# Six instead of seven gate tiles in the first phase of an S5 + SwiGLU kernel

## The chip, the cores and the metric

The kernel runs on one core of one Trainium2 chip. The metric is device time in microseconds of one execution; the time before is the median of three runs. One execution was also profiled, and all readings of the trace come from that one.

## The reference, cut to what matters

For x of 1 x 2048 x 512 in bf16, the kernel computes a layernorm and two branches on it, a state-space scan (S5) and a SwiGLU feed-forward with F = 1376:

```python
xn = _layernorm(x, axis=-1)
return x + _A_ref(xn, ...) + _B_ref(xn, w_gate, w_up, w_down)
# _B_ref
g = _silu(x @ w_gate)
u = x @ w_up
return (g * u) @ w_down
```

`_A_ref` multiplies xn by a complex matrix (512 x 512), runs the recurrence h = Lam_bar * h + Bu along the 2048 tokens, multiplies by C, and adds xn * Dskip. What the change touches is the gate product of the first 512 tokens and the layernorm of these tokens.

## The kernel before, in words

The tokens are cut into four chunks of 512, and a chunk into four token tiles of 128. F is cut into ten tiles of 128 and a rest of 96; tiles go in pairs (`FP`, L710), so a chunk has five gate pairs and five up pairs. Each pair takes a pair of PSUM banks: two times four matmuls of 512 columns (one for each 128 rows of the contraction, `ffn_mm`, L714) fill it, and one instruction of ScalarE (ACT) reads it, a silu for gate (`silu_pair`, L726) or a copy for up (`ffn_up`, L779). There are eight banks, so four pairs. `next_pair` (L374) hands them out in rotation: it skips a pair that is reserved, and one in which TensorE (PE) has written and nobody is yet recorded as its reader (`_bank_live`, L369).

The work is put down as tasks with the tiles that they read and write, and a planner makes the order when the program is built. PE and the DMA queue of SyncE (SP) keep the order in which the code adds their tasks (`_CHAIN`). ACT, VectorE (DVE) and GpSimd (POOL) are sorted by a list planner (`_schedule`) by estimated times (`est`), with extra orders where `order` or `od` gives them. Waits follow from the tiles; a bank counts as a whole, so a task that writes a bank waits for all who read it before.

The first phase handles chunk 0 while x and the weights are still coming in; later chunks get their transposes by DMA and are not touched. `ffn_gate_quarters([0, 1, 2, 3])` (L742) does this:

- Four bank pairs are reserved for eight gate tiles. The last bank (7) is taken off the list for transposes (`xt_pair`, L746); seven tiles remain, in banks 0 to 6. Gate tile 6's bank also takes warm-up matmuls on constants (`pe_warm`) and the first transpose.
- `ln_chunk0` (L513) puts one chain on DVE for token tiles 0 to 3: statistics of 128x512 (L517), aggregate (L518), then a root on ACT (L519), reciprocal (L524), and xn (`ln_apply`, L500). Before tile 3's reciprocal stands a small transpose of parameters (L522).
- `xt_tile` (L543) transposes xn of a token tile on PE in four blocks of 128 (L548) and copies them to `xnT`: on ACT in three copies for tiles 0 to 2 (L559), on DVE in two for tile 3 (L557). Tile 1's blocks are transposed two and two, into the same bank 7; tiles 2 and 3 in one go of four.
- For each token tile q, the k slices (contraction rows) are taken in groups, and within a group all seven gate tiles get a matmul of 128 columns for each slice (L763). The table `place` (L754) says ahead of which of these the transposes of the next token tile stand. Tile q = 3 goes in two groups of two slices.
- ACT's order of roots and copies is written out (`seq`, L769): sd0, ev0_0, ev0_1, sd1, ev0_2, ev1_0, ev1_1, sd2, ev1_2, ev2_0, ev2_1, sd3, ev2_2 (sd is a root, ev a copy of transposes). Then ACT loads the silu table (`act_table`, L772).
- Gate tile 7 follows as four 512-column matmuls in bank 7 (L774), then the four silu pairs are put down.

After it the code adds three up pairs of chunk 0, the fifth gate pair, two more up pairs, and the rest of the kernel. The first up pair takes banks 0 and 1, which the first silu reads.

The gate weights come as four loads, one for each k slice, of the columns of the first-phase tiles (`wg_load`, L424; `FG = NQ * 128`, L416), two on SP's queue (slices 1 and 3) and two on ACT's (0 and 2). The other gate columns come in one load (`ld_wg1`, L441) on SP behind the first up load. `wres` (L705) makes a gate tile from number `NQ` on wait for that load.

Of the kernel before, what the change touches and what calls it, by code (L numbers as in the profile page):

```python
# [14 lines left out]
AF = mybir.ActivationFunctionType  # L15
# [235 lines left out]
def bass_parallel_sum__ssm_conv_s5__swiglu_ffn__prompt_kernel(  # L251
# [28 lines left out]
    EPS = 1e-5  # L280

    g = _Graph()
    es = ExitStack()
    with es:
# [9 lines left out]
        x_sb = sb("x_sb", [128, NT, D], B16)  # L294
# [33 lines left out]
        st = sb("st", [128, 8, 6], F32)  # L328
# [45 lines left out]
        def next_pair():  # L374
            for _ in range(NB // 2):
                b = 2 * (pair_ctr[0] % (NB // 2))
                pair_ctr[0] += 1
                if not (b in reserved or _bank_live(b) or _bank_live(b + 1)):
                    return b
            raise AssertionError("all PSUM pairs live")  # L380
# [31 lines left out]

        TILEB = 128 * D * 2
        FH0 = 6 * 128
        NQ = 7
        FG = NQ * 128  # L416

        def pload(name, slot, src, **kw):
# [54 lines left out]
        def pe_warm(n, w=512, bk=None):  # L473
            if bk is None:
                bk = next_pair()

            def mm(e, bk=bk):
                for _ in range(n):
                    inst = e.matmul(pbank[:, bk, 0:w], lhsT=one.to_broadcast([128, 128]), rhs=one.to_broadcast([128, w]), start=True, stop=True)  # L479
                return inst  # L480
            g.add("pe", mm, writes=BK(bk), name="pe_warm", est=n * w * 0.84, ninst=n)
# [17 lines left out]
        def ln_apply(a, order=()):  # L499
            return g.add("dve", lambda e: e.tensor_scalar(out=xn_sb[:, a % NXN, :], in0=x_sb[:, a, :], scalar1=mv[:, a, 0:1], scalar2=rstd[:, a:a + 1],  # L500
                                                          op0=ALU.subtract, op1=ALU.mult),
                         reads=[("x", a), ("mv", a), ("rstd", a)], writes=[("xn", a % NXN)], name="xn%d" % a, est=350, order=order)
# [8 lines left out]
        hold = {}  # L511

        def ln_chunk0():  # L513
            last = None
            for a in range(4):
                order = (last,) if last else ()
                last = g.add("dve", lambda e, a=a: e.bn_stats(out=st[:, a, :], in_=x_sb[:, a, :]), reads=[("x", a)], writes=[("st", a)], name="bnst%d" % a, est=640, order=order)  # L517
                last = g.add("dve", lambda e, a=a: e.bn_aggr(out=mv[:, a, :], in_=st[:, a, :]), reads=[("st", a)], writes=[("mv", a)], name="bnag%d" % a, est=160, order=(last,))  # L518
                hold["sd%d" % a] = g.add("act", lambda e, a=a: e.activation(out=sd0[:, a:a + 1], in_=mv[:, a, 1:2], func=AF.Sqrt, bias=EPS),  # L519
                                         reads=[("mv", a)], writes=[("sd0", a)], name="sd%d" % a, est=190)  # L520
                if a == 3:
                    last = g.add("dve", lambda e: e.transpose(out=prT[:], in_=prow[:]), reads=[("prow", k) for k in range(3)] + [("prow0",)],  # L522
                                 writes=[("praw", k) for k in range(3)], name="parT", est=90, order=(last,))
                last = g.add("dve", lambda e, a=a: e.reciprocal(out=rstd[:, a:a + 1], in_=sd0[:, a:a + 1]), reads=[("sd0", a)], writes=[("rstd", a)],  # L524
                             name="rstd%d" % a, est=140, order=(last,))
                last = ln_apply(a, (last,))
            hold["xn3"] = last

        def ln_chunk(c):
            for a in range(4 * c, 4 * c + 4):  # L530
# [7 lines left out]
                for a in range(4 * c, 4 * c + 4):  # L538
                    ln_apply(a)

        xt_pair = [None]

        def xt_tile(a, k0, k1, slot=None):  # L543
            slot = xt_pair[0] if slot is None else slot

            def tr(e):
                for k in range(k0, k1):
                    inst = e.transpose(out=ptr[:, slot, k * 128:(k + 1) * 128], in_=xn_sb[:, a, k * 128:(k + 1) * 128], identity=ident[:])  # L548
                return inst
            g.add("pe", tr, reads=[("xn", a), ("ident",)], writes=BK(slot), name="xT%d_%d" % (a, k0), est=(k1 - k0) * 64, ninst=k1 - k0)  # L550
            src = ptr[:, slot, 0:512].rearrange("p (k t) -> p k t", k=KT)
            for q0, q1 in ((0, 2), (2, 4)) if a == 3 else ((0, 1), (1, 2), (2, 4)):
                if q0 < k0 or q1 > k1:
                    continue
                rd = dict(reads=BK(slot), writes=[("xnTq", a, k) for k in range(q0, q1)] + ([("xnT", 0, a)] if q1 == KT else []), name="xTev%d_%d" % (a, q0))
                if a == 3:
                    t = g.add("dve", lambda e, q0=q0, q1=q1: e.tensor_copy(out=xnT[0][:, a, q0:q1, :], in_=src[:, q0:q1]), est=320, order=(hold["xn3"],), **rd)  # L557
                else:
                    t = g.add("act", lambda e, q0=q0, q1=q1: e.activation(out=xnT[0][:, a, q0:q1, :], in_=src[:, q0:q1], func=AF.Identity), est=130 + 110 * (q1 - q0), **rd)  # L559
                hold["ev%d_%d" % (a, q0)] = t  # L560
# [153 lines left out]
        def ffn_mm(c, i, which, bk):  # L714
            fs = fsz[i]
            w = wg if which == "g" else wu

            def mm(e, bk=bk, w=w, i=i, fs=fs, c=c):
                for kt in range(KT):
                    inst = e.matmul(pbank[0:fs, bk, :].rearrange("p (j t) -> p j t", j=4), lhsT=w[:, kt, i * 128:i * 128 + fs], rhs=xnT[c][:, :, kt, :],  # L720
                                    start=(kt == 0), stop=(kt == KT - 1))
                return inst
            g.add("pe", mm, reads=wres("wg" if which == "g" else "wu", i) + [("xnT", c, j) for j in range(4)],
                  writes=BK(bk), name="mm_%s%d_%d" % (which, c, i), est=4 * 216, ninst=4)
# [10 lines left out]
        def ffn_gate(c, ip):  # L735
            i0, n = FP[ip]
            bk = next_pair()
            for k in range(n):
                ffn_mm(c, i0 + k, "g", bk + k)
            silu_pair(c, ip, bk)  # L740

        def ffn_gate_quarters(pairs):  # L742
            banks = {ip: next_pair() for ip in pairs}
            reserved.update(banks.values())
            tiles = [(2 * ip + k, banks[ip] + k) for ip in pairs for k in range(2)]
            xt_pair[0] = tiles.pop()[1]  # L746
            wbank = tiles[-1][1]
            pe_warm(8, 512, wbank)
            pe_warm(2, 128, wbank)
            ln_chunk0()  # L750
            xt_tile(0, 0, 1, wbank)
            xt_tile(0, 1, 4)
            pe_warm(1, 256, tiles[-2][1])
            place = {(0, 2, 4): (1, 0, 2), (1, 0, 3): (1, 2, 4), (1, 2, 2): (2, 0, 4), (2, 2, 2): (3, 0, 4)}  # L754
            for q in range(4):
                for k0, k1 in (((0, 1), (1, 2), (2, 3), (3, 4)), ((0, 1), (1, 2), (2, 4)), ((0, 1), (1, 2), (2, 4)), ((0, 2), (2, 4)))[q]:
                    for n, (i, bk) in enumerate(tiles):
                        if (q, k0, n) in place:
                            xt_tile(*place[(q, k0, n)])

                        def mm(e, bk=bk, i=i, q=q, k0=k0, k1=k1):
                            for kt in range(k0, k1):
                                inst = e.matmul(pbank[:, bk, q * 128:(q + 1) * 128], lhsT=wg[:, kt, i * 128:(i + 1) * 128], rhs=xnT[0][:, q, kt, :],  # L763
                                                start=(kt == 0), stop=(kt == KT - 1))
                            return inst
                        g.add("pe", mm, reads=[("wg", "k%d" % k) for k in range(k0, k1)] + [("xnTq", q, k) for k in range(k0, k1)], writes=BK(bk),
                              name="mm_gq%d_%d_%d" % (i, q, k0), est=(k1 - k0) * 56, ninst=k1 - k0)
            reserved.clear()
            seq = ["sd0", "ev0_0", "ev0_1", "sd1", "ev0_2", "ev1_0", "ev1_1", "sd2", "ev1_2", "ev2_0", "ev2_1", "sd3", "ev2_2"]  # L769
            for a_, b_ in zip(seq, seq[1:]):  # L770
                hold[b_].od.add(hold[a_])
            act_table(AF.Silu, (hold["ev2_2"],))  # L772
            hold["evac"] = g.tasks[-1]
            ffn_mm(0, NQ, "g", xt_pair[0])  # L774
            for ip in pairs:
                silu_pair(0, ip, banks[ip])
            hold["evac"] = [t for t in g.tasks if t.name == "silu0_0"][0]

        def ffn_up(c, ip):  # L779
            i0, n = FP[ip]  # L780
# [180 lines left out]
            dc_A(c0 + 1, 3, 416, 96, bk)  # L961
            dc_B(c0 + 1, 3, 416, 96, bk, 1)

        ffn_gate_quarters([0, 1, 2, 3])
        params_a()
        tables()
        params_b()
# [91 lines left out]
```

## Time and profile before

| what | value |
|---|---|
| median of 3 runs | 178.13 us (177.83 to 178.2) |
| the profiled execution | 178.16 us |
| its span, first to last instruction | 176.3 us |
| busy: PE, DVE, ACT, POOL | 98%, 92%, 47%, 6% |
| first-phase matmuls (L763) | 112, of 128 columns each, 5.3 to 12.9 us |
| first silu (L732) | starts at 12.53 us |
| later gate and up matmuls (L720) | 512 columns, from 12.89 us on |

All times within the trace count from the start of the span. A line of the timeline has the start, the duration, the engine (PEld is PE's weight load), the line of the code, the operation, the output and inputs by name, the shape, how many instructions are merged, and in brackets the idle time before with what ended it. `pb` is a PSUM bank, `wgu` the gate and up weights, `sg` the silu's output, `st`, `mv`, `sd`, `rstd` the steps of the layernorm. The chain of waits is the work that ended last, followed back from the end: at each step what released it. A line of it has start, duration, engine, tile and line.

### The profile page before, as it was taken

How to read it: one execution, taken by the hardware profiler on the slowest of the kernel's cores; microseconds unless marked ns; L12 is line 12 of the kernel's file. 1: busy time of each engine (PE TensorE's matmuls, PEld its weight loads, DVE VectorE, ACT ScalarE, POOL GpSimd, SP SyncE). 2: the span in 40 equal slices, each digit the busy share in tenths (PEclk: the TensorE clock that was granted, in tenths of full speed). 3: DMA queues.
4: the chain of work that ended last, by engine and by line, in shares of the span. 5: the costliest groups of instructions: out<-in, count | busy, mean ns of one | idle time of the engine just before them, and what ended most of it. 6: DMA issues, size and time to landing. Idle time of an engine off the chain costs nothing.

```text
span 176.3 us, 2474 instructions
## 1 busy us (share of the span) xinstructions
PE 173.0 (98%) x954; PEld 85.7 (49%) x962; DVE 161.7 (92%) x279; ACT 83.6 (47%) x113; POOL 10.8 (6%) x21
## 2 busy tenths in 40 slices
PE   8999999999999999999999999999999999999995
PEld 2894444444444496444444444444444444444443
DVE  2773999999999999999999999999999999999933
ACT  3469989799999767100356564000265620000000
POOL 3040500127000000000000000000000000000000
PEclk9999999999999999999999999999999999999999
DMA  5996665654685101023240000001100000000122
GB/s 162 272 372 163 129 125 172 154 115 86 119 289 121 32 0 30 4 60 100 54 130 0 4 0 0 0 0 59 63 0 0 0 0 0 0 4 0 59 89 89
DMA packets 26246, 13.48 MB, mean 76 GB/s; under 512 B 18460, under 2 KB 26108, under 8 KB 26236
## 3 DMA queue, kind: packets, MB, share of 16 engines
q1 hardware_dynamic: 25916, 12.89, 27.5%
q10 hardware_dynamic: 320, 0.46, 0.7%
q8 instruction: 7, 0.11, 0.3%
q14 instruction: 3, 0.02, 0.0%
HBM read 6.85 MB, written 2.10 MB: 51 GB/s over the span
## 4 chain that ended last, share of the span: by engine, by line
PE 96%; ACT 1%; ACTq 1%; issue 1%; DVE 0%
PE pb L720 36%; PE pb L908 19%; PE pb L837 16%; PE pb L922 16%; PE pb L763 4%; PE pb L802 3%; PE pb L919 1%; PE pb L954 1%; ACTq L405 1%; ACT L468 1%; PE pb L548 1%; DVE xn_sb L500 0%; ACT sm L468 0%; DVE x_sb L926 0%; PE pb L479 0%
## 5 line engine op out<-in xcount | busy, mean ns | idle before, releaser
L720 PE MATMUL pb<-xnT,wgu 128*128 128x512 bf16 x212 | 46.2, 379 | 0.0
L877 DVE TENSOR_TENSOR_SCAN rot<-sm,car,rot 128x512 bf16<-128x512 f32 x32 | 38.8, 1266 | 0.0
L732 ACT ACTIVATE sg<-pb 128x1024 bf16<-128x1024 f32 x20 | 20.1, 1023 | 34.9 <-PE pb L720 33.8
L908 PE MATMUL pb<-wd,hT 128*128 128x512 bf16 (+2 forms) x166 | 34.5, 366 | 0.2
L720 PEld LDWEIGHTS pb<-xnT,wgu 128*128 128x128 bf16 x212 | 20.7, 98 | 24.8 <-ACT sg L732 0.2
L922 PE MATMUL pb<-W,hss 128*128 128x512 bf16 (+2 forms) x132 | 28.6, 366 | 0.3 <-issue 0.2
L908 PEld LDWEIGHTS pb<-wd,hT 128*128 128x128 bf16 x170 | 16.2, 98 | 18.5
L789 ACT ACTIVATE uf<-pb 128x1024 bf16<-128x1024 f32 x20 | 20.5, 1024 | 7.4 <-PE pb L720 6.3
L837 PE MATMUL pb<-xnT,BT 128*128 128x512 bf16 x96 | 21.0, 379 | 0.0
L922 PEld LDWEIGHTS pb<-W,hss 128*128 128x128 bf16 x136 | 12.8, 98 | 15.1 <-issue 0.4
L844 ACT ACTIVATE u_sb<-pb 128x1024 bf16<-128x1024 f32 x16 | 16.3, 1022 | 5.6 <-PE pb L837 5.2
L720 PE MATMUL pb<-scrC,wgu 128*128 128x512 bf16 x80 | 17.4, 379 | 0.0
L837 PEld LDWEIGHTS pb<-xnT,BT 128*128 128x128 bf16 x96 | 9.4, 98 | 11.3
L926 DVE TENSOR_TENSOR x_sb<-pb,x_sb 128x512 bf16<-128x512 f32 (+2 forms) x17 | 11.0, 653 | 4.1 <-PE pb L922 4.0
L791 DVE TENSOR_TENSOR hT<-sg,uf 128x1024 bf16<-128x1024 bf16 x20 | 13.5, 683 | 0.4 <-ACT uf L789 0.3
L720 PEld LDWEIGHTS pb<-scrC,wgu 128*128 128x128 bf16 x80 | 7.8, 98 | 9.4
L484 DVE BATCH_NORM_STATS2 st<-x_sb 128x6 f32<-128x512 bf16 x12 | 7.4, 679 | 2.7 <-DMA x_sb<-in_A_x_dram 2.7
L868 DVE TENSOR_TENSOR rot<-u_sb,cosT 128x2048 bf16<-128x2048 bf16 x8 | 9.8, 1220 | 0.0
L868 DVE TENSOR_TENSOR rot<-rot,sin 128x2048 bf16<-128x2048 bf16 x8 | 9.8, 1220 | 0.0
L868 DVE TENSOR_TENSOR rot<-u_sb,sin 128x2048 bf16<-128x2048 bf16 x8 | 9.7, 1218 | 0.0
L868 DVE TENSOR_TENSOR rot<-rot,cosT 128x2048 bf16<-128x2048 bf16 x8 | 9.7, 1213 | 0.0
L868 DVE TENSOR_TENSOR hss<-rot 128x2048 bf16<-128x2048 bf16 x8 | 9.5, 1219 | 0.0
(79 smaller groups left out, 147.9 us busy)
## 6 DMA issues: line engine op xcount, KB each, us to landing
out_dram<-x_sb SPq DMA_DIRECT2D x15, 128.0 KB, 1.7
x_sb<-in_A_x_dram SPq DMA_DIRECT2D x3, 512.0 KB, 4.4
wd<-in_B_w_down_dram SPq DMA_DIRECT2D x1, 1280.0 KB, 6.3
wgu<-in_B_w_up_dram SPq DMA_DIRECT2D x1, 768.0 KB, 5.8
wgu<-in_B_w_up_dram SPq DMA_DIRECT2D x1, 608.0 KB, 8.0
x_sb<-in_A_x_dram SPq DMA_DIRECT2D x4, 128.0 KB, 3.7
wgu<-in_B_w_gate_dram SPq DMA_DIRECT2D x1, 480.0 KB, 6.6
wgu<-in_B_w_gate_dram ACTq DMA_DIRECT2D x2, 224.0 KB, 4.0
```

Source lines behind the costliest of these rows:

```text
L484: return g.add("dve", lambda e, a=a: e.bn_stats(out=st[:, a % 8, :], in_=x_sb[:, a, :]), reads=[("x", a)], writes=[("st", a % 8)], name="b ...
L720: inst = e.matmul(pbank[0:fs, bk, :].rearrange("p (j t) -> p j t", j=4), lhsT=w[:, kt, i * 128:i * 128 + fs], rhs=xnT[c][:, :, kt, :], sta ...
L732: g.add("act", lambda e: e.activation(out=sg[rows, sl, 0:n, :].rearrange("p a t -> p (a t)"), in_=pair_f32(rows, bk, 512 * n), func=AF.Sil ...
L789: g.add("act", lambda e: e.activation(out=uf[rows, ul, 0:n, :].rearrange("p a t -> p (a t)"), in_=pair_f32(rows, bk, 512 * n), func=AF.Ide ...
L791: g.add("dve", lambda e: e.tensor_tensor(out=hT[rows, hb, i0:i0 + n, :], in0=sg[rows, sl, 0:n, :], in1=uf[rows, ul, 0:n, :], op=ALU.mult), ...
L837: inst = e.matmul(pbank[:, bk, :].rearrange("p (j t) -> p j t", j=4), lhsT=BT[:, ri, kt, pt * 128:(pt + 1) * 128], rhs=xnT[c][:, :, kt, :] ...
L844: g.add("act", lambda e: e.activation(out=u_sb[:, us].rearrange("p r t -> p (r t)"), in_=pair_f32(slice(0, 128), b0), func=AF.Identity), r ...
L868: tt = lambda out, a, b, op, r, w, nm: g.add("dve", lambda e: e.tensor_tensor(out=out, in0=a, in1=b, op=op), reads=r, writes=w, name="%s_% ...
L877: g.add("dve", lambda e, A0=A0, A1=A1, k=k, ri=ri, pt=pt: e.tensor_tensor_scan(out=A1[:, k, ri, :], data0=rr[:, pt:pt + 1].to_broadcast([1 ...
L908: inst = e.matmul(pbank[:, bk, 0:nc_], lhsT=hT[:, hb, i, lt * 128:(lt + 1) * 128], rhs=wd[:, i, c0:c0 + nc_], start=(i == 0), stop=False)
L922: inst = e.matmul(pbank[:, bk, 0:nc_], lhsT=hss[:, hb, pt, ri, lt * 128:(lt + 1) * 128], rhs=W12[:, ri, pt, c0:c0 + nc_], start=False, sto ...
L926: g.add("dve", lambda e: e.tensor_tensor(out=x_sb[:, a, c0:c0 + nc_], in0=pbank[:, bk, 0:nc_], in1=x_sb[:, a, c0:c0 + nc_], op=ALU.add), r ...
```

## The change

- `NQ` is 6: the four gate loads carry 768 columns instead of 896, and `ld_wg1` 608 instead of 480.
- The phase reserves three pairs for six gate tiles (banks 0 to 5), and the fourth pair for transposes: `wbank` (bank 7) and `tp` (bank 6). Tile 1's four transposes go together into bank 7, ahead of the fifth gate tile in slice 2 of q = 0; tile 2's go into bank 6, tile 3's into bank 7.
- In the layernorm chain, tile 3's statistics are two halves of 256 columns, the first ahead of tile 2's reciprocal and the second behind tile 2's xn; the aggregate takes both.
- Gate tiles 6 and 7 are computed as an ordinary pair of 512-column matmuls (`ffn_gate(0, 3)`), put down after the three silu pairs.

```diff
-        NQ = 7
+        NQ = 6
...
+            stats(2, 2, 0, 512)
+            aggr(2, 2, 1)
+            stats(3, 4, 0, 256)
+            norm(2)
+            stats(3, 5, 256, 512)
+            aggr(3, 4, 2)
+            dve(lambda e: e.transpose(out=prT[:], in_=prow[:]), [("prow", k) for k in range(3)] + [("prow0",)], [("praw", k) for k in range(3)], "parT", 90)
+            norm(3)
...
         def ffn_gate_quarters(pairs):
             banks = {ip: next_pair() for ip in pairs}
+            tp = next_pair()
             reserved.update(banks.values())
+            reserved.add(tp)
             tiles = [(2 * ip + k, banks[ip] + k) for ip in pairs for k in range(2)]
-            xt_pair[0] = tiles.pop()[1]
-            wbank = tiles[-1][1]
+            wbank = tp + 1
             pe_warm(8, 512, wbank)
             pe_warm(2, 128, wbank)
             ln_chunk0()
             xt_tile(0, 0, 1, wbank)
-            xt_tile(0, 1, 4)
-            pe_warm(1, 256, tiles[-2][1])
-            place = {(0, 2, 4): (1, 0, 2), (1, 0, 3): (1, 2, 4), (1, 2, 2): (2, 0, 4), (2, 2, 2): (3, 0, 4)}
+            xt_tile(0, 1, 4, tp)
+            pe_warm(1, 256, tiles[-1][1])
+            place = {(0, 2, 4): (1, 0, 4, wbank), (1, 2, 2): (2, 0, 4, tp), (2, 2, 2): (3, 0, 4, wbank)}
...
             act_table(AF.Silu, (hold["ev2_2"],))
             hold["evac"] = g.tasks[-1]
-            ffn_mm(0, NQ, "g", xt_pair[0])
             for ip in pairs:
                 silu_pair(0, ip, banks[ip])
             hold["evac"] = [t for t in g.tasks if t.name == "silu0_0"][0]
+            ffn_gate(0, len(pairs))
...
-        ffn_gate_quarters([0, 1, 2, 3])
+        ffn_gate_quarters([0, 1, 2])
```

`stats`, `aggr` and `norm` are the same instructions as before, each ordered behind the one before it on DVE; `ffn_gate(c, ip)` (L735) takes `next_pair()`, two `ffn_mm` and the silu.

More of the change, by code (lines that the diff above doesn't have):

```diff
@@ L513, in ln_chunk0 @@
         def ln_chunk0():
[L514 to L519, printed above, removed]
-                                         reads=[("mv", a)], writes=[("sd0", a)], name="sd%d" % a, est=190)
[L521 to L526, printed above, removed]
@@ L527, in ln_chunk0, with dve, stats, aggr @@
-            hold["xn3"] = last
+            chain = [None]
+            def dve(fn, reads, writes, name, est):
+                t = g.add("dve", fn, reads=reads, writes=writes, name=name, est=est, order=(chain[0],) if chain[0] else ())
+                chain[0] = t
+                return t
+            def stats(a, slot, c0, c1):
+                dve(lambda e: e.bn_stats(out=st[:, slot, :], in_=x_sb[:, a, c0:c1]), [("x", a)], [("st", slot)], "bnst%d_%d" % (a, c0), 100 + (c1 - c0) * 1.05)
+            def aggr(a, s0, n):
+                hold["bnag%d" % a] = dve(lambda e: e.bn_aggr(out=mv[:, a, :], in_=st[:, s0:s0 + n, :].rearrange("p s v -> p (s v)")), [("st", s0 + j) for j in range(n)], [("mv", a)], "bnag%d" % a, 160)
+                hold["sd%d" % a] = g.add("act", lambda e: e.activation(out=sd0[:, a:a + 1], in_=mv[:, a, 1:2], func=AF.Sqrt, bias=EPS),
+                                         reads=[("mv", a)], writes=[("sd0", a)], name="sd%d" % a, est=190)
@@ new lines, in norm @@
+            def norm(a):
+                dve(lambda e: e.reciprocal(out=rstd[:, a:a + 1], in_=sd0[:, a:a + 1]), [("sd0", a)], [("rstd", a)], "rstd%d" % a, 140)
+                chain[0] = hold["xn%d" % a] = ln_apply(a, (chain[0],))
+            stats(0, 0, 0, 512)
+            aggr(0, 0, 1)
+            norm(0)
+            stats(1, 1, 0, 512)
+            aggr(1, 1, 1)
+            norm(1)
+            stats(2, 2, 0, 512)
+            aggr(2, 2, 1)
+            stats(3, 4, 0, 256)
+            norm(2)
@@ L539, in ln_chunk, with xt_tile @@
                     ln_apply(a)
-        xt_pair = [None]
-        def xt_tile(a, k0, k1, slot=None):
-            slot = xt_pair[0] if slot is None else slot
+        def xt_tile(a, k0, k1, slot):
             def tr(e):
```

## The prediction

> **What bounds the kernel now.** I read the chain that ended last first, then the first 14 us in order of time, engine by engine, then the waits and the DMA landings there. From the page and from the chain in order of time:
>
> ```profile
> PE 96%; ACT 1%; ACTq 1%; issue 1%; DVE 0%
> ...
> 5.49 0.72 PE pb L763 x7
> ...
> 10.93 2.12 PE pb L763 x38
> 13.05 11.22 PE pb L720 x52
> 24.28 13.81 PE pb L837 x64
> ```
>
> TensorE (PE) sets the end. The pieces join without a hole from 6.31 us on: 38 128-column matmuls in 2.12 us are 0.056 us each, 64 of 512 columns in 13.81 us are 0.216 us each. So a PE microsecond added or idled near 13 us is paid in full at the end, unless something later has slack on PE, and the largest "issue" piece after 13 us is 0.16 us. VectorE (DVE) is 92% busy, but its last hss is written at 160.7 us and PE reaches the matmuls that first need it near 167 (160.25, then 32 matmuls at 0.216): some 6 us of cover.
>
> The change lies before 13.7 us. In order of time there:
>
> ```profile
> 6.28 0.63 PEld L763 LDWEIGHTS pb<-xnT,wgu 128*128 128x128 bf16 x11 [0.29 <-ACT xnT L559]
> 6.61 0.69 DVE L517 BATCH_NORM_STATS2 st<-x_sb 128x6 f32<-128x512 bf16 x1 [0.29 <-DMA x_sb<-in_A_x_dram]
> 7.34 0.18 DVE L518 BATCH_NORM_AGGREGATE mv<-st 128x2 f32<-128x6 f32 x1
> 8.00 0.41 DVE L500 TENSOR_SCALAR xn_sb<-x_sb,mv,rstd 128x512 bf16<-128x512 bf16 x1
> 8.70 0.27 PEld L548 LDWEIGHTS pb<-ident,xn_sb 128*128 128x128 bf16 x4
> 9.18 0.45 ACT L559 ACTIVATE xnT<-pb 128x128 bf16<-128x128 bf16 x2 [0.71 <-PE pb L548]
> 9.51 0.21 ACT L519 ACTIVATE sd<-mv 128x1 f32<-128x1 f32 x1
> 9.75 0.16 DVE L524 RECIPROCAL rstd<-sd 128x1 f32<-128x1 f32 x1 [0.37 <-ACT sd L519]
> 9.95 0.41 DVE L500 TENSOR_SCALAR xn_sb<-x_sb,mv,rstd 128x512 bf16<-128x512 bf16 x1
> 10.49 0.26 PEld L548 LDWEIGHTS pb<-ident,xn_sb 128*128 128x128 bf16 x4
> 10.97 0.49 DVE L557 COPY xnT<-pb 128x256 bf16<-128x256 bf16 x2 [0.61 <-PE pb L548]
> 12.53 3.77 ACT L732 ACTIVATE sg<-pb 128x1024 bf16<-128x1024 f32 x4 [0.94 <-PE pb L763]
> 12.84 0.58 PEld L720 LDWEIGHTS pb<-xnT,wgu 128*128 128x128 bf16 x4
> 13.61 10.18 PEld L720 LDWEIGHTS pb<-xnT,wgu 128*128 128x128 bf16 x48 [0.18 <-ACT sg L732]
> ```
>
> The reader is to see three things. The layernorm chain of tile 3 (statistics, root on ScalarE (ACT), xn, transposes, copies) ends just as PE has run through its other work: with seven gate tiles PE never waits long for it. The first silu starts at 12.53, and gate tile 7 (12.84) fills PE until that silu, 1.02 us long, gives up banks 0 and 1 to the first up pair at 13.61. And the wait before 6.28 is named after an ACT copy that was done at 5.95; the weights of k-slice 1 landed at 6.17, so it is their DMA.
>
> **The change part by part.** The profiled execution took 178.16 us (span 176.3 us and 1.9 around it), 0.03 over the median of 178.13. My mark is the start of the first up matmul. Before: 12.89 (the trace's start of gate tile 7's first matmul) + 4 x 0.216 = 13.75.
>
> *Loads.* The four gate loads shrink from 224 to 192 KB. In the trace's packets 1,792 bytes took 74 ns, 1,536 bytes 65 ns; a load is 8 packets on each of 16 engines, so 0.07 us saved per load. Landings before: slice 1 6.17, x tile 2 6.59, slice 3 7.16, x tile 3 7.45. After: about 5.97 (three loads share the way), 6.37, 6.87, 7.16. Between no gain and one by bytes (0.1 us more) I take the packets. The later gate load grows to 608 KB, rows of 1,216 for 960 bytes: 32 packets an engine at 53 for 44 ns, +0.29 us, what the four saved; it lands at 12.67 as before and is needed at 13.1. Count and order of SP's and ACT's DMAs stay.
>
> *Tile 1's transposes together.* Gone is the wait of the second two for the copies of the first two in the same bank (7.73 behind copies of 7.23 to 7.68). PE starts slice 1 at 6.08; 10 matmuls, transposes at 6.62. From the first of four transposes to its first copy the rows give 0.48 us (8.70 to 9.18): copies 7.10 to 7.38 and to 7.55. PE by then has four transposes and 8 matmuls behind it, 7.30; it waits for the first copy and 0.05 us of hand-over until 7.43, a stall of 0.13 that the seventh tile covered. Then 16 matmuls: 8.33.
>
> *Statistics.* Tile 2's start at 6.39 instead of 6.61 and end, with the aggregate, at 7.30; its root goes behind the copies on ACT, 7.43 to 7.63. The first half of tile 3's statistics (128x256) is put into that wait. No row has this shape: it lies between 0.18 us (aggregate row) and 0.69 (128x512). I take 0.43, in between because of the fixed part, so 7.33 to 7.76: xn of tile 2 ends at 8.29 against 8.41. At 0.69 everything behind is 0.27 us later; at 0.18 nothing is gained, the root is late next. Transposes of tile 2: 8.34, copies 8.82 to 9.27. The second half and the two-set aggregate (0.18 to 0.69, I take 0.2, the nearest row) end at 8.86, beside the transposes; at 0.69 they cost 0.24. Late next is the order on ACT: tile 3's root stands behind the second copy of tile 2, 9.15 to 9.36. Its xn ends at 10.00 (before 10.36).
>
> *Six tiles.* PE: transposes and 8 matmuls until 9.01, stall until the copy at 9.15, 16 matmuls until 10.05, tile 3's transposes at 10.06, 8 matmuls until 10.73, stall until the copy (10.54 to 10.83) is handed over at 10.88, 24 matmuls until 12.22. So 16 matmuls (0.90 us) are gone and the phase starts 0.2 earlier, but it ends only 0.62 earlier than 12.84: the rest went into stalls.
>
> *The pair.* Gate tiles 6 and 7 take the fifth bank pair handed out: of four pairs that is pair 0 again, and its first silu must have read it. So the change adds a wait, in front of everything on PE. Tile 1's last matmul starts at 10.88 + 15 x 0.056 = 11.72; from that to the silu the trace has 0.31 (12.22 to 12.53): silu 12.03 to 13.05 (the second ACT table load is over by about 11.2). PE idles from 12.22 to 13.10, 0.88 us, with nothing queued that may pass. First matmul 13.12, eight at 0.216: the first up matmul at 14.85. Sum: 14.85 - 13.75 = **+1.10 us**. In parts: -0.62 (phase end) + 0.88 (wait) + 0.86 (tile 6 now behind the phase); the rest is rounding. The up pairs then move on by one pair each (banks 2, 4, 6), free long before PE reaches them (second silu over by 14.0); nothing there wins the time back.
>
> The list planner sorts ACT and DVE anew. Its price lies between 0 (the 6 us of cover) and one pair eviction that PE would wait for, 1.02 us (silu row); I take 0.
>
> *The clock.* The seven matmuls from 5.49 run at 0.103 us each, those from 10.93 at 0.056: PE works at half speed at first and turns to full just after 6 us, though the page's clock row shows full speed throughout. No idle time of PE near 0.9 us occurs after that, so the rows cannot say whether a stall brings half speed back. [...]
>
> **The rivals.** *No wait for the silu* (the pair turns out to be the free transpose banks): gate tile 6 starts at 12.24, up at 13.97, +0.22, 178.4 us. For it: banks 6 and 7 are free from 11.03. Against: the pair is chosen by rotation when the program is built, and a pair whose silu is already recorded counts as free.
>
> *Faster*: PE stays dense from 6.08 (90 matmuls and 12 transposes, 5.71 us, end at 11.79) and meets no silu wait: first pair matmul 11.81, up at 13.54, -0.21, 177.9 us; with slice 1 landing another 0.2 earlier, 177.7. It decides only if the pair is free and tile 3's first copy ends by 10.39 (24 matmuls before 11.79, and the hand-over) instead of 10.83. For it: weights and x tiles come earlier, and DVE's idle 0.29 and 0.37 us are used. Against: xn of tile 2 and 3 each hang on a root on ACT that stands behind copies.
>
> *The clock falls in the new stall*: the first stretch at half speed lasted from 0.83 to about 6.03; 5.2 us of it lose 2.6: +3.7 us, 181.8. For it: it is the longest idle of PE in the run. Against: nothing but that the 0.29 us wait at 6 us did not hinder the turn to full speed.
>
> **How the numbers follow.** Forecast 0.82: 178.13 + 1.10 = 179.2. No silu wait 0.08, faster 0.05 (of it 0.02 below 177.77), clock 0.05. The forecast's own range is 178.9 (hand-overs and loads 0.3 better) to 179.9 (0.27 + 0.24 of the two unknown statistics and a little of the planner's 1.02). Tails included, I reach down to the first rival: 178.4 to 179.9. A measurement can tell about 0.2%, 0.36 us. Faster by more: 0.02. Within (first rival at +0.2, and most of the second): 0.08 + 0.03 = 0.11. Slower by more: 0.82 + 0.05 = 0.87.
>
> **What would show it.** Right: in the chain the last quarter matmuls end near 12.2, then the 512-column matmuls start near 13.1 with an idle of some 0.9 us put down to ACT sg; 8 gate matmuls ahead of the first up; silu at about 12.0, alone in its wait; from there all as before, about 1.1 later. The half statistics show 0.43 us; three stalls of 0.1 to 0.2 before 11 us. Wrong: gate tile 6 without a wait, a phase end before 11.9 or after 12.6, matmul steps at 0.43 us after 13 us, or new waits of PE behind DVE or ACT later.

## The result and the profile after

The changed kernel takes 179.18 us (179.0 to 179.37, six runs) beside 178.16 us for the kernel before on the same chip (177.83 to 178.35, six runs): 1.02 us more, a ratio of 1.0054 with a 95% interval of 1.0041 to 1.0067. The prediction was 179.2.

The profiled execution of the changed kernel took 179.37 us with a span of 177.4. In it the functions have moved down by 15 or 16 lines: L779 is the first-phase matmul (L763 before), L735 the gate and up matmul (L720), L747 the silu (L732), L563 the transposes (L548), L574 the copies on ACT (L559), L853 the B matmuls (L837). The chain of waits in order of time:

```profile
6.93 0.22 PE pb L563 x4
7.15 1.44 PE pb L779 x24
...
10.26 0.23 PE pb L563 x4
10.49 1.47 PE pb L779 x24
11.98 1.03 ACT sg L747
13.02 0.05 issue
13.06 12.26 PE pb L735 x56
25.32 13.81 PE pb L853 x64
```

Before, PE alone made this chain from 6.31 us on. Now a silu of ACT stands in it from 11.98 to 13.01. By the timeline the first 512-column matmul starts 0.17 us later than before (13.06 for 12.89), and there are 56 instead of 52 of them up to the B matmuls, which is 4 x 0.216 = 0.86 us. (The chain has the start of before at 13.05, since it counts a matmul only from the end of the one ahead of it; the same 0.17 us shows there as 12.26 us for 56 matmuls, where e1 below, without an idle, has 12.09.) So the B matmuls come at 25.32 instead of 24.28, and after that the two chains run alike: the last piece on PE before the end starts at 175.21 instead of 174.16. The whole difference, 1.04 us, is made before 25.4 us.

PE's weight loads between 11 and 14.5 us and ACT between 11 and 16.5 us, from the timeline:

```profile
10.95 1.27 PEld L779 LDWEIGHTS pb<-xnT,wgu 128*128 128x128 bf16 x22
13.06 1.41 PEld L735 LDWEIGHTS pb<-xnT,wgu 128*128 128x128 bf16 x8 [0.84 <-ACT sg L747]
```
```profile
11.98 2.85 ACT L747 ACTIVATE sg<-pb 128x1024 bf16<-128x1024 f32 x3 [0.71 <-PE pb L779]
15.00 1.02 ACT L747 ACTIVATE sg<-pb 128x1024 bf16<-128x1024 f32 x1 [0.16 <-PE pb L735]
```

The phase's last weight load ends at 12.22 (10.95 + 1.27), and nothing follows on PE until the first silu is done, 0.84 us later. The fourth silu, in a row with the others before, now waits for the new pair.

The layernorm chain and the transposes, from the timeline, as they answer to the lines of before:

```profile
7.22 0.18 DVE L525 BATCH_NORM_AGGREGATE mv<-st 128x2 f32<-128x6 f32 x1
7.35 0.43 DVE L522 BATCH_NORM_STATS2 st<-x_sb 128x6 f32<-128x256 bf16 x1
...
7.96 0.41 DVE L500 TENSOR_SCALAR xn_sb<-x_sb,mv,rstd 128x512 bf16<-128x512 bf16 x1
8.29 0.42 DVE L522 BATCH_NORM_STATS2 st<-x_sb 128x6 f32<-128x256 bf16 x1
8.42 0.23 PEld L563 LDWEIGHTS pb<-ident,xn_sb 128*128 128x128 bf16 x4
...
8.74 0.21 DVE L525 BATCH_NORM_AGGREGATE mv<-st 128x2 f32<-128x12 f32 x1
8.86 0.45 ACT L574 ACTIVATE xnT<-pb 128x128 bf16<-128x128 bf16 x2 [0.86 <-PE pb L563]
...
9.19 0.20 ACT L526 ACTIVATE sd<-mv 128x1 f32<-128x1 f32 x1
```

The first half of tile 3's statistics runs in DVE's wait for the root of tile 2, the second behind tile 2's xn, and the aggregate of tile 3 ends at 8.95. But its root on ACT starts at 9.19, behind the copies of 8.86, as ACT's order has it.

### The profile page after: what moved, and what is told of

The parts are those of the page before. It is cut to its first block, busy times and chain, and to the rows that moved or that the text cites. A ratio compares the mean times of both kernels' runs of the same rounds, so it can differ in the third digit from the quotient of the medians.

```text
span 177.4 us, 2451 instructions
## 1 busy us (share of the span) xinstructions
PE 173.3 (98%) x942; PEld 85.0 (48%) x950; DVE 161.5 (91%) x280; ACT 83.3 (47%) x113; POOL 10.5 (6%) x21
## 4 chain that ended last, share of the span: by engine, by line
PE 95%; DMA 1%; DVE 1%; ACT 1%; issue 0%
PE pb L735 36%; PE pb L924 19%; PE pb L853 16%; PE pb L938 15%; PE pb L779 3%; PE pb L818 3%; DMA x_sb<-in_A_x_dram 1%; PE pb L935 1%; PE pb L970 1%; PE pb L563 1%; ACT sg L747 1%; DVE st L522 0%; DVE xn_sb L500 0%; DVE x_sb L942 0%; PE pb L479 0%
## 5 line engine op out<-in xcount | busy, mean ns | idle before, releaser
L735 PE MATMUL pb<-xnT,wgu 128*128 128x512 bf16 x216 | 47.1, 379 | 0.7 <-ACT sg L747 0.7
L747 ACT ACTIVATE sg<-pb 128x1024 bf16<-128x1024 f32 x20 | 20.2, 1022 | 35.8 <-PE pb L735 35.0
L735 PEld LDWEIGHTS pb<-xnT,wgu 128*128 128x128 bf16 x216 | 21.1, 98 | 26.1 <-ACT sg L747 0.8
L853 PE MATMUL pb<-xnT,BT 128*128 128x512 bf16 x96 | 21.0, 379 | 0.0
L735 PE MATMUL pb<-scrC,wgu 128*128 128x512 bf16 x80 | 17.4, 379 | 0.0
L853 PEld LDWEIGHTS pb<-xnT,BT 128*128 128x128 bf16 x96 | 9.4, 98 | 11.4
L735 PEld LDWEIGHTS pb<-scrC,wgu 128*128 128x128 bf16 x80 | 7.8, 98 | 9.4
L884 DVE TENSOR_TENSOR rot<-rot 128x2048 bf16<-128x2048 bf16 x8 | 9.7, 1218 | 0.0
```

The costliest lines, as they stand in the source:

```text
L747: g.add("act", lambda e: e.activation(out=sg[rows, sl, 0:n, :].rearrange("p a t -> p (a t)"), in_=pair_f32(rows, bk, 512 * n), func=AF.Sil ...
L853: inst = e.matmul(pbank[:, bk, :].rearrange("p (j t) -> p j t", j=4), lhsT=BT[:, ri, kt, pt * 128:(pt + 1) * 128], rhs=xnT[c][:, :, kt, :] ...
L884: tt = lambda out, a, b, op, r, w, nm: g.add("dve", lambda e: e.tensor_tensor(out=out, in0=a, in1=b, op=op), reads=r, writes=w, name="%s_% ...
```

## The experiments

Theory: the loss is PE's wait for the first silu, which gives the pair its banks; the time that the shorter phase gains is less than this wait and the tile that moved behind it. Rivals: the wait is swallowed later; it is the end of the phase, the statistics, the transposes or the loads that count. Each kernel was timed in turns with the kernel before on one chip, e1 to e4, e5 to e8, and e9 and e10 on a chip each; the median of the kernel before was 177.94 us beside e1 to e4, 178.18 beside e5 to e8, and 177.90 beside e9 and e10.

**e1: the pair in the free banks.** In `ffn_gate_quarters`:

```diff
+            pair_ctr[0] = 3
             ffn_gate(0, len(pairs))
```

> The changed kernel, but gate tiles 6 and 7 take the transpose banks (6 and 7), which nobody reads after 11.0 us. Theory (PE's wait for the first silu, 0.88 us in the changed kernel's trace, is paid in full): the pair starts right behind the phase near 12.2, its eight matmuls are over by 13.95, and the first up pair finds banks 0 and 1 already read at 13.0; 179.18 - 0.85 = 178.3 us, still 0.15 to 0.25 over the kernel before. Rival (the wait only moves to the next matmuls, or the later work has slack that swallowed it): 179.2 us, with an equal wait further on.

Measured: 178.36 us, ratio 1.0022 (1.0012 to 1.0031). Its chain of waits has no silu in it:

```profile
10.15 0.23 PE pb L563 x4
10.38 1.90 PE pb L779 x32
12.28 12.09 PE pb L735 x56
24.37 5.83 PE pb L854 x27
```
```profile
12.06 2.53 PEld L735 LDWEIGHTS pb<-xnT,wgu 128*128 128x128 bf16 x13
```

The pair's weight loads (L735) start at 12.06 with no idle ahead of them. The B matmuls begin at 24.37 instead of 25.32, of which 0.11 comes from an earlier phase (its first silu starts at 11.87). Counted from tile 3's transposes, 10.15 here and 10.26 in the changed kernel, they begin 14.22 and 15.06 us later: the wait was worth 0.84 us. By the medians it was 0.82, by the two ratios 0.57 (the kernel before was 0.22 faster beside e1 than beside the changed kernel); each way most of the loss goes with it. What stays, 0.42 us over the kernel before by the medians, has the sign of the prediction's first rival (+0.22): the phase gives up a tile's work and ends only two thirds of that earlier (0.62 us of 0.90 in the changed kernel).

**e2: a later silu to wait for.**

```diff
+            pair_ctr[0] = 5
             ffn_gate(0, len(pairs))
```

> The changed kernel, but the pair takes banks 2 and 3, so it waits for the second silu, which ends 0.92 us after the first (13.92 for 13.01). Theory: PE's wait grows from 0.88 to 1.80 us and all of it shows: 179.18 + 0.92 = 180.1 us. Rival (PE's lateness is partly taken back by later work, as ACT has less to do then): 179.2 to 179.7. If a longer idle let the clock fall, matmul steps of 0.43 us would follow and 181 us or more.

Measured: 180.22 us, ratio 1.0123 (1.0106 to 1.0139). In its chain two silus lie between the phase and the pair, and PE's weight loads were idle for 1.76 us:

```profile
9.99 0.23 PE pb L563 x4
10.22 1.47 PE pb L779 x24
11.69 0.02 issue
11.71 1.95 ACT sg L747 x2
13.66 0.05 issue
13.71 12.26 PE pb L735 x56
25.97 4.10 PE pb L854 x19
```
```profile
13.70 0.76 PEld L735 LDWEIGHTS pb<-xnT,wgu 128*128 128x128 bf16 x5 [1.76 <-ACT sg L747]
```

The 0.92 us more of wait cost 1.04 by the medians. Nothing later took it back. The 56 matmuls after it need 12.26 us, 0.219 each, as in the changed kernel: the clock did not fall.

**e3: the first silu earlier, with the phase as long as it is.** The steps of the last token tile are sorted so that gate tiles 0 and 1 come first:

```diff
+                steps = [(k, n) for k in ks for n in range(len(tiles))]
+                if q == 3:
+                    steps.sort(key=lambda s: s[1] >= 2)
```

> The changed kernel, but in the last token tile gate tiles 0 and 1 get all four slices before tiles 2 to 5 get any. The phase on PE ends as before (12.2), but the first silu can start at 10.87 + 7 x 0.056 + 0.31 = 11.58 instead of 11.98, and the second copy of tile 3 (ends near 11.0) is in time. Theory: silu to 12.60, pair at 12.65 instead of 13.06, 179.18 - 0.41 = 178.8 us. Rival (it is the phase's end or the later silus that count, not the first silu): 179.2 us.

Measured: 178.62 us, ratio 1.0035 (1.0023 to 1.0048). PE's weight loads are idle for 0.39 us:

```profile
10.09 0.23 PE pb L563 x4
...
24.70 5.39 PE pb L857 x25
```
```profile
12.44 2.06 PEld L735 LDWEIGHTS pb<-xnT,wgu 128*128 128x128 bf16 x11 [0.39 <-ACT sg L747]
```

The four kernels with the same pair of tiles give a line: idle weight loads ahead of the pair of 0, 0.39, 0.84 and 1.76 us go with 178.36, 178.62, 179.18 and 180.22 us. That is 1.86 us of time for 1.76 us of wait. The traces say it more sharply. From tile 3's transposes to the B matmuls the four take 14.22, 14.61, 15.06 and 15.98 us, which is 0, 0.39, 0.84 and 1.76 more than e1, the idle times to the hundredth; from the B matmuls to the last piece on PE all four take 149.88 or 149.89 us. The wait for the silu that frees the banks is paid in full, and it is this silu's end that counts, not the phase's.

**e4: the statistics as before.** `ln_chunk0` of the kernel before in the changed kernel.

> The changed kernel with the layernorm chain of the kernel before (tile 3's statistics whole, behind tile 2's xn). Reading of the trace: tile 3's root stands on ACT behind the second copy of tile 2 (9.19), and whole statistics would have its input ready at 9.22; so the halves bought only some 0.04 us: 179.2 us. Rival, nearer to the prediction (the half hidden in DVE's wait is worth its 0.43 us, as the chain of tile 3 sets the phase's end): 179.5 to 179.6 us.

Measured: 179.21 us, ratio 1.009 (1.0056 to 1.0125; one run of 181.51 makes it wide, the other six lie from 179.12 to 179.54). Against the kernel before it is 1.27 us over by the medians, where the changed kernel is 1.02 over, so the times alone do not exclude a loss of some 0.25 us. The timeline shows that the halves bought next to nothing:

```profile
7.68 0.41 DVE L500 TENSOR_SCALAR xn_sb<-x_sb,mv,rstd 128x512 bf16<-128x512 bf16 x1
8.00 0.69 DVE L517 BATCH_NORM_STATS2 st<-x_sb 128x6 f32<-128x512 bf16 x1
8.58 0.45 ACT L555 ACTIVATE xnT<-pb 128x128 bf16<-128x128 bf16 x2 [0.86 <-PE pb L544]
8.72 0.18 DVE L518 BATCH_NORM_AGGREGATE mv<-st 128x2 f32<-128x6 f32 x1
8.94 0.20 ACT L519 ACTIVATE sd<-mv 128x1 f32<-128x1 f32 x1
```

Whole statistics of 0.69 us and the aggregate are over at 8.90, just when ACT has started tile 2's two copies and comes to the root. From tile 2's xn to the first silu it is 4.05 us here (7.68 to 11.73) and 4.02 in the changed kernel (7.96 to 11.98). The rival's 0.4 us are not in the trace.

**e5: tile 1's transposes two and two again.**

```diff
-            place = {(0, 2, 4): (1, 0, 4, wbank), ...
+            place = {(0, 2, 4): (1, 0, 2, wbank), (1, 0, 3): (1, 2, 4, wbank), ...
```

> The changed kernel, but tile 1's transposes two and two in the same bank, at the places they had before. Theory: the second two wait for the copies of the first two, the last copy of tile 1 ends near 8.3 instead of 8.0, tile 2's transposes start about 0.17 later than 8.42 and with them all that follows: 179.3 to 179.4 us. Rival (tile 2's xn, ready at 8.37, sets that start anyway, so the split is hidden): 179.2 us.

Measured: 179.22 us, ratio 1.0066 (1.0049 to 1.0083), not to be told from the changed kernel's 1.0054. In the trace tile 2's transposes start at 8.27, 0.12 us behind the end of xn at 8.15, where the changed kernel has 0.05 (8.42 behind 8.37). So the split costs about 0.1 us at most in these two traces, and not the 0.17 of the expectation. The rival, no change, is nearer, though not by its own reason: in e5 it is PE's own matmuls, and not xn, that set this start.

**e6: the gate loads as wide as before.**

```diff
-        FG = NQ * 128
+        FG = 7 * 128
...
-            if nm == "wg" and i < NQ:
+            if nm == "wg" and i < 7:
```

> The changed kernel, but the four gate loads carry 896 columns as before (the second gate load 480). Theory: slice 1, x tile 2 and slice 3 land 0.1 to 0.2 us later; the phase starts and tile 2's statistics run that much later, some of it caught by PE's stalls: 179.2 to 179.4 us. Rival (the loads do not matter once six tiles leave PE waiting): 179.2, no change. Other rival (each landing is paid in full): 179.4 or more.

Measured: 179.25 us, ratio 1.0069 (1.0051 to 1.0086): 0.07 over the changed kernel by the medians, less than these runs resolve. Between "no change" and 0.2 the run does not decide; the median speaks against a loss paid in full (179.4 or more), the interval alone does not exclude it. In its trace slice 1 lands at 6.21, PE waits for it, and the B matmuls begin at 25.46, 0.14 later than in the changed kernel's; these are two single executions.

**e7 and e8: the parts that keep the seventh tile.** The kernel before with the new layernorm chain (e7), and with it and tile 1's transposes together in bank 7 (e8: `place = {(0, 2, 4): (1, 0, 4), (1, 2, 2): (2, 0, 4), (2, 2, 2): (3, 0, 4)}`).

> The kernel before (seven tiles, gate tile 7 in the transpose bank) with the new layernorm chain alone. Theory: PE is dense there, so an earlier xn of tiles 2 and 3 has nothing to give but the 0.08 and 0.02 us of waits behind their copies: 178.1 us. Rival (the chain of tile 3 bounds the phase before as well): 177.8 us.

> The kernel before with the new layernorm chain and tile 1's four transposes together in its one transpose bank, ahead of the fifth gate tile: the parts of the change that do not give up the seventh tile. Theory: at most the waits of 0.26 us that PE has in the phase, of which two (0.08 before tile 1's last slices, 0.02) can go: 178.0 to 178.1 us, hardly told from 178.16. Rival (tile 2 and 3 earlier by 0.2 let the whole phase move): 177.8 us.

Measured: 178.03 us, ratio 0.9996 (0.9981 to 1.0011), and 177.90 us, ratio 0.9993 (0.9977 to 1.0009). Neither can be told from the kernel before. The rival's 0.3 us would be 0.998; it lies at the lower end of both intervals, just outside e7's and just inside e8's. In e8's profiled execution, the slowest of its twelve with 178.89 us, the chain shows a load come late that the prediction's steps had in time:

```profile
6.04 7.34 DMA wgu<-in_B_w_gate_dram
13.38 0.05 issue
13.43 0.60 PE pb L739 x2
```

The second gate load landed at 13.38, and gate tile 7 waited for it, with PE's weight loads idle for 0.41 us. With seven tiles its landing has little cover (12.67 for 12.84 in the kernel before).

**e9 and e10: seven tiles with narrower first loads.** Both have e8's layernorm chain and transposes. The slices' loads carry 768 columns, gate tile 6's 128 columns come in one load behind x tile 3, and tile 6 takes its four slices of a token tile in one go, inside the next token tile (in the last token tile it goes along with the others); e10 adds e3's order.

```diff
+        FG = 6 * 128
+        FG1 = NQ * 128
...
+        dma("ld_wg6", wg[:, :, FG:FG1], wg_v[:, :, FG:FG1], [("wg", 6)], 512 * (FG1 - FG) * 2)
...
+            steps += [(1, 0, 1, n) for n in six] + [(0, 0, 4, 6)] + [(1, 1, 2, n) for n in six]
```

> A version built from what the runs showed: seven tiles in the phase and gate tile 7 in the transpose bank, as in the kernel before, with the new layernorm chain and tile 1's transposes together, but the four gate loads carry 768 columns and gate tile 6's 128 columns come in one load behind x tile 3. Tile 6 takes its four slices of a token tile at once, late in the next token tile, where six tiles alone left PE waiting 0.13 to 0.15 us. Theory: slice 1 lands at 5.3 to 6.1 instead of 6.2, the six tiles start up to 0.35 us earlier, tile 6 fills the stalls, the last token tile is bound by tile 3's copies (10.9 + 28 matmuls = 12.45 instead of 12.84), up at about 13.3 instead of 13.54: 177.8 us, ratio 0.998. Rival (the start is set by x tile 0 and the layernorm chain, or tile 6's load is late near 7.4 and blocks PE): 178.1 us or more.

> As e9, and in the last token tile gate tiles 0 and 1 get all slices first, so that the first silu ends before gate tile 7's four matmuls do. Theory: in e9 up 0 waits for the silu until about 13.2, and that sets it; here the silu ends near 12.8 and up follows gate tile 7 at once: 0 to 0.1 us under e9, 177.7 to 177.8 us. Rival (e9's up does not wait for the silu): no difference.

Measured: 177.90 us, ratio 0.9992 (0.9977 to 1.0008), and 177.92 us, ratio 1.0001 (0.999 to 1.0011). No version is measurably faster than the kernel before; the 0.998 expected of e9 is within its interval, but the median does not show it. The chain of e9's profiled execution has a reason in its first lines:

```profile
1.71 4.61 DMA wgu<-in_B_w_gate_dram
6.32 0.14 issue
6.45 0.38 PE pb L794 x4
...
10.73 2.23 PE pb L794 x40
12.96 1.08 PE pb L743 x5
```

It begins with the load of slice 2, landed at 6.32: narrower, and hardly earlier than before, where it took 4.7 us from its issue at 1.7. PE is dense from 6.45 with the same work, and the 512-column matmuls start at 12.96 for 13.05. In e10 the first silu starts earlier than in e9 (11.96 for 12.44), and the 0.19 us for which e9's weight loads wait for it ahead of the first up matmul are gone; but the 52 matmuls take 11.22 us in both, so that wait had cost PE nothing, as e10's rival says.

## Why the prediction was right, point by point

**The bound.** PE set the end before and after, and no later slack took anything back: from the B matmuls to the last piece on PE it is 149.89 us after and 149.88 before, and e2's longer wait came through whole. The planner sorted some of the table work on ACT and DVE anew; by the same figures it cost nothing, as taken.

**The wait and its size.** Predicted: phase end 12.22, silu 12.03, pair 13.10, a wait of 0.88. Measured: 12.22, 11.98, 13.06, 0.84 by the idle row. The sum was +1.10; the chains differ by 1.04 and the medians by 1.02. The right reading was that of the bank rotation: the fifth pair handed out is pair 0, although banks 6 and 7 had been free from about 11 us. e1 to e3 show that it was this wait.

**The phase.** Steps predicted and measured in the changed kernel: xn of tile 2 at 8.29 and 8.37, root of tile 3 at 9.15 and 9.19, half statistics 0.43 and 0.43 us, two-set aggregate 0.2 and 0.21. The stalls that the seventh tile had covered came where they were put, but shorter than the 0.13 to 0.15 us taken: 24 weight loads in 1.48 us twice and 32 in 1.94, where starts 0.056 us apart and 0.098 us for the last load would be 1.39 and 1.83, so 0.09, 0.09 and 0.11. That the phase ended at 12.22 to the hundredth is luck. The first steps came 0.1 us late (tile 1's transposes 6.71 for 6.62), and the steps from transposes to first copy were shorter than taken for tiles 2 and 3 (0.44 for 0.48 us); in e1 to e5, with the same six tiles and loads, the phase's last weight load ends anywhere from 11.9 to 12.1. That the root of tile 3 would be late next, behind ACT's copies, was part of the working; e4's trace shows that because of it the halves are worth next to nothing for tile 3 (4.05 for 4.02 us).

**The loads were mis-sized, with little effect.** The term was 0.07 us per load from packet times, slice 1 at 5.97 instead of 6.17, the second gate load at 12.67. In the changed kernel's execution the load of slice 1 took 4.4 us from issue to landing (6.1), in e1's and e2's, with the same loads, 3.6 (5.3). The spread between executions, 0.8 us, is four times the 0.2 that the term gave for this load. But e1's first silu came only 0.11 us earlier, and these 0.11 us are there from tile 1's transposes on (6.60 for 6.71): in both executions PE was busy with the six matmuls of slice 0 at half speed (median 314 ns in the changed kernel) until about 6 us, and DVE with tile 1's xn until 6.48, so of the 0.8 us little more than 0.1 could show. In e2, with e1's landing but matmuls at full speed from about 5.6 on, the first silu came at 11.71. The second gate load landed at 11.8 (5.8 us from its issue), well ahead of its use. A price by packets cannot show such spreads; it was this cover that made them harmless.

**Tile 1's transposes** were counted within the phase, without a gain of their own; e5's trace puts it at 0.1 us or less.

**The rivals.** "No wait" was priced at +0.22, and e1, which makes it true, lies 0.42 over the kernel before by the medians, 0.21 to 0.55 by its interval. The faster case was nowhere near: e1 had the free pair and slice 1 0.8 us earlier than the changed kernel, and still tile 3's first copy ended at 10.71, where this case needed 10.39. The clock did not fall after 0.84 us of idle nor after e2's 1.76: behind each the 56 matmuls of 512 columns took 12.26 us, 0.219 each. Nor did it fall after the changed kernel's three stalls of about 0.1 us: behind them the matmuls of 128 columns start 0.056 us apart again. In the slow first stretch of the kernel before, these steps are 0.43 and 0.103 us. What a longer idle does was not shown.

**Left open.** How much of the loss e1 leaves: 0.42 us by the medians, but only 0.09 by the two profiled executions at the B matmuls (24.37 for 24.28), in which the phase starts at times of its own. And whether narrower loads are worth 0 or 0.1 us here.

## What to carry to other kernels

Before a fill-in piece of work is taken out of a phase, look at what it hides behind it: gate tile 7 cost PE nothing extra because it ran (12.89 to 13.75 us) while a silu (12.53 to 13.55) freed the next banks, and a pair that needs these same banks cannot take over that job. Follow the buffer rotation by hand when the number of buffers in a phase changes; one free pair existed and was not the one handed out. And a step hidden in a wait pays only if the next thing in the chain is not held by another engine's fixed order, as tile 3's root was here (4.02 us with the halves, 4.05 without).

## What the runs showed of the hardware that was not expected

- The same loads in the same place land up to 0.8 us apart in different executions: slice 1, 192 KB, 4.4 us from issue to landing in the changed kernel, 3.6 in e1 and e2, 3.8 in e9.
- PE's turn from half to full speed (matmuls of 128 columns 0.103 and 0.056 us apart in the kernel before) came at different times in these runs, with the same warm-up in the code (from 0.82 us on in the changed kernel). Around 5.6 us the changed kernel's matmuls still have the long form, e10's the short one (median 314 and 219 ns). In e5 the transposes, of the same shape, have it at 4.8 us (219; 314 in the changed kernel), so the turn moves by more than 1 us:

```profile
L779 PE MATMUL pb<-xnT,wgu x5: 289/314/314, 5.5 to 5.9; 128*128 128x128 bf16 x5
```
```profile
L794 PE MATMUL pb<-xnT,wgu x6: 219/219/230, 5.4 to 5.7; 128*128 128x128 bf16 x6
```
```profile
L563 PE MATMUL pb<-ident,xn_sb x4: 219/219/229, 4.8 to 5.0; 128*128 128x128 bf16 x4
```

- Statistics of 256 columns take 0.43 us, of 512 columns 0.69: halving the width saves 38%, and two halves cost 0.16 us more than one whole.
